# A three-layer kernel on one core: when the side parts of a weight conversion are issued, the order of joined results, and the queue of the row stores

## The chip, the cores and the metric

The kernel runs on one core of one Trainium2 chip. The metric is the device time of one execution in microseconds (us). Before the change it is 578.14 us, the median of three runs (577.61 to 579.5). The profile that is read below comes from one further execution, which took 581.89 us; its span, from the first to the last instruction, is 580.0 us.

## The reference

Three stages follow each other on 1536 tokens of width 512 (two batches of 768). All inputs but the two integers are float32.

```python
scores = q @ k.T / 8 - slope[h] * dist        # 8 heads of width 64, window of 96 + 8 global keys
x = softmax(where(keep, scores, -1e9)) @ v    # [1536, 512]
h = x @ moe_w_in                              # [512, 2048]
x = where(h > 0, h, exp(min(h, 0)) - 1) @ moe_w_out          # [2048, 512]
h = maximum(maximum(x @ moe2_w1, x @ moe2_w2), x @ moe2_w3)  # each [512, 768]
out = h @ moe2_w_out                          # [768, 512]
```

The weights reach the kernel as float64. The kernel turns them into float32 by bit operations and splits each into a high part (a rounded copy) and a low part (the rest), and three matmuls (high by high, high by low, low by high) make one product.

## The kernel before, in words

**Stages.** The tokens go in three blocks of 512 through attention and the first feed-forward layer (`run`). Attention of a later block runs beside the matmuls of the block in front of it. In `run`, the loop over `fc` (16 pieces of 128 hidden columns) does for each `fc`: `product` (12 matmuls into a PSUM bank `h`, L636), the ELU on ACT and DVE (ACT relu and exp, L656 and L657; DVE max, L661), a high part on ACT (`gh`, L643), a low part on DVE (`gl`, L648), and then the out product of the `fc` before it (`out_high`, L667, eight matmuls that read `gh`, and `out_low`, L675, four that read `gl`). So `gh` of one `fc` has the time of one out product and one product (24 matmuls) before PE needs it. The last block has no attention beside it.

**The second layer** (`second`) makes three passes, `p` = 0 to 2. A pass has three keys, `q` = 0 to 2 (the three matrices of the maximum), and then the rows of the out product. A key has `pair` (blocks 0 and 1 joined: seven products of six matmuls each, L905, with sums of operands formed before, in the manner of Strassen and Winograd; results are put together by DVE adds and maxima, `result`, L925 to L934) and `single` (block 2 alone: two products of twelve matmuls, L636). At `q` = 2 each of the six gate tiles is closed: `closed` makes a high part on ACT (L915) and a low part on DVE (L916). Then `rows` goes over 12 rows of 128 tokens: six matmuls each (L997, they read the closed tiles, for rows 0 to 3 the tiles (0,0) and (0,1)), then an ACT copy (pass 0, L1003) or a DVE add of the partial sum of the pass before (L1005), and a store. The partial row is loaded three rows ahead (`fetch`, L986). Row tiles and open gate tiles share seven buffers: row 0 follows on a row of the pass before, rows 1 to 6 each on one gate tile in the order (1,1), (0,0), (0,1), (1,0), (2,0), (2,1), and row 7 and later on the stores of rows 0 and later. PE's products go round eight PSUM banks (`bank`).

**The weight conversion for the second layer** is a generator, `pieces`. Each `next` runs it up to a `yield`, a piece. For each of the 12 groups there are two raw tiles. For a tile: `w_first` (an ACT rescale in place, L475, and a DVE shift, L476), two `w_word` (DVE, L485, each reads what the rescale wrote), `w_split` (ACT high part, L495, and a POOL low part, L496). Three of four groups then form sums: `w_sums` 0 and 1 (two DVE adds each, L508 to L512), with ACT high parts (L515) and POOL low parts (L516) of both. A group of the first kind has 8 pieces, of the other kind 6, 90 in all. Raw tiles come by SP into three buffers; the second raw tile of a group goes into the buffer that the POOL low part of the first sums (L516) of the group before leaves.

**Where pieces are drawn.** In `run`, from `fc` = 9 of the last block: one before the max L661, three at the end of each `fc`, 28 in all. In `second`, by `work(n)` between products, the first four of which are parts of `late` (the split of block 2's tokens, L616 and L617).

Each engine takes its instructions in the order of the program; an ACT instruction that waits for DVE holds all behind it.

```python
e = self.elu_exp(h, n)            # ACT, ACT
...                               # before: a piece here
self.elu_max(e, h)                # DVE
gh = self.high(e, n)              # ACT
gl = self.low(e, gh, n, ...)      # DVE
...                               # pieces here
```

Of the kernel before, what the change touches and what calls it, by code (L numbers as in the profile page):

```python
# [11 lines left out]
F32 = mybir.dt.float32  # L12
F32R = mybir.dt.float32r
# [4 lines left out]
ALU = mybir.AluOpType  # L18
# [5 lines left out]
P = 128  # L24
# [362 lines left out]
class Feed:  # L387
# [80 lines left out]

    def w_first(self, j):

        if j not in self.wraw:
            return
        r = self.wraw[j]
        a = r[:, :, 1].bitcast(F32)
        self.nc.scalar.activation(a, a, AF.Copy, scale=2.0 ** -112)  # L475
        self.nc.vector.tensor_scalar(  # L476
            r[:, :, 0], r[:, :, 0], 29, 1, op0=ALU.logical_shift_right, op1=ALU.bitwise_or
        )

    def w_word(self, j, n):  # L480
        if j not in self.wraw:
            return
        t, a = self.wraw[j][:, :, 0], self.wraw[j][:, :, 1]
        c, op = ((3, ALU.logical_shift_left), (0x80000000, ALU.bitwise_and))[n]
        self.nc.vector.scalar_tensor_tensor(t, a, c, t, op0=op, op1=ALU.bitwise_or)  # L485

    def w_split(self, j):
        if j not in self.wraw:
            return
        nc = self.nc  # L490
        v = self.wraw.pop(j)[:, :, 0].bitcast(F32)
        if j % 2 == 0:
            self.w[j // 2] = self.wt.tile([P, 2, 2, 512], F32R, tag="w", name="w")
        w = self.w[j // 2]
        nc.scalar.copy(w[:, j % 2, 0], v)  # L495
        nc.gpsimd.tensor_tensor(  # L496
            w[:, j % 2, 1], v, w[:, j % 2, 0].bitcast(F32), op=ALU.subtract
        )

    def w_sums(self, j, n):  # L500


        nc = self.nc
        r0, r1 = self.raws[j], self.raws[j + 1]
        v0, v1, t0, t1 = (r[:, :, i].bitcast(F32) for i in (0, 1) for r in (r0, r1))
        a, b = slice(0, 256), slice(256, 512)
        if n == 0:
            nc.vector.tensor_tensor(t1[:, a], v1[:, a], v1[:, b], op=ALU.add)  # L508
            nc.vector.tensor_tensor(t0[:, a], v0[:, a], v1[:, a], op=ALU.subtract)
            return  # L510
        nc.vector.tensor_tensor(t1[:, b], t1[:, a], v0[:, a], op=ALU.subtract)
        nc.vector.tensor_tensor(t0[:, b], v0[:, b], t1[:, b], op=ALU.subtract)  # L512
        w = self.s[j // 2] = self.wt.tile([P, 2, 2, 512], F32R, tag="w", name="ws")
        for u, t in enumerate((t0, t1)):
            nc.scalar.copy(w[:, u, 0], t)  # L515
            nc.gpsimd.tensor_tensor(w[:, u, 1], t, w[:, u, 0].bitcast(F32), op=ALU.subtract)  # L516

    def pieces(self):


        for i in range(2 * NJ):
            j = 2 * (NFC + i)
            while self.nl < min(j + 3, 2 * NFC + 4 * NJ):
                self.w_load()
            self.raws = {j + u: self.wraw[j + u] for u in range(2)}
            for u in range(2):
                self.w_first(j + u)
                yield
                self.w_word(j + u, 0)
                yield  # L530
                self.w_word(j + u, 1)
                self.w_split(j + u)
                if u == 0 or i % 4 == 3:
                    yield
            if i % 4 < 3:
                yield
                self.w_sums(j, 0)
                yield
                self.w_sums(j, 1)
                yield  # L540
            self.made.add(NFC + i)

    def operands(self, y0, y1):
# [183 lines left out]
    def run(self, at, k, x=None, h0=None, aside=None):  # L727
# [3 lines left out]
        nc, ps = self.nc, self.ps  # L731
        nblk = len(BLOCKS)
# [6 lines left out]
        for bi, n in enumerate(BLOCKS):  # L739
            prev = y = None  # L740
            for fc in range(NFC):
                tag = ("h", "S0")[fc % 2] if k >= len(at.steps) + 2 else "h"
# [14 lines left out]
                if bi == nblk - 1 and fc == 2:  # L757
                    sums = self.operands(ysave[0], ysave[1])
# [15 lines left out]
                else:  # L774
# [3 lines left out]
                        at.turn_pe(k - 1)  # L778
                    if not due:
                        at.turn_act(k - 1, nc.scalar.copy)  # L780
                if bi == nblk - 1 and fc > 1:
                    next(sums if fc < 9 else conv, None)
                self.elu_max(e, h)
                if bi == 0:
                    self.c_low(fc + 3)
                if fc == NFC - 1 and bi + 1 < nblk:
                    x = self.split_tiles()
                    t = at.take(g0)
# [37 lines left out]
                    self.c_rebase(fc + 3)  # L826
                    self.w_ahead(min(2 * fc + 4, 2 * NFC - 1))
                if bi == nblk - 1 and fc > 1:
                    for _ in range(1 if fc < 9 else 3):
                        next(sums if fc < 9 else conv, None)  # L830
                k += 1
                prev = gh, gl
            if bi + 1 < nblk:
                self.split_part(x, t, 0, 2, 2, nc.vector)
                for i in range(1, BLOCKS[bi + 1] // GRP):
                    t = at.take(g0 + i)
# [3 lines left out]
            if bi == nblk - 2:  # L840
# [5 lines left out]
                conv = self.pieces()  # L846
# [72 lines left out]
    def pair(self, key, q, g, left, work):  # L919


        nc, o, w, s = self.nc, self.o, self.w[key], self.s[key]
        def add(t, u, tag, pool=self.act):
            out = pool.tile([P, 512], F32, tag=tag, name=tag)
            nc.vector.tensor_tensor(out, t, u, op=ALU.add)  # L925
            return out

        def result(t, u, b, j):
            m = self.gate(g, b, j)
            if q == 0:  # L930
                nc.vector.tensor_tensor(m, t, u, op=ALU.add)
            else:
                c = add(t, u, "c", self.m2)
                nc.vector.tensor_tensor(m, c, m, op=ALU.max)  # L934

        p1 = self.part(w, 0, 0, o["b11"])
        if left:
            self.out_low(*left)
        e1 = self.act.tile([P, 512], F32, tag="e", name="e1", bufs=1)
        nc.scalar.copy(e1, p1)  # L940
        if left:
            self.late = self.save(left[0], left[3])
        p6 = self.part(s, 1, 256, o["t2"])
        u2 = add(p6, e1, "gl")
        work(1)
        p5 = self.part(s, 1, 0, o["t1"])
        v = add(p5, u2, "gh")
        work(1)
        p7 = self.part(s, 0, 0, o["t3"])
        u3 = add(p7, u2, "gl")  # L950
        result(p5, u3, 1, 1)
        result(self.part(w, 0, 256, o["b21"]), e1, 0, 0)
        result(self.part(w, 1, 256, o["t4"]), u3, 0, 1)
        result(self.part(s, 0, 256, o["b22"]), v, 1, 0)
        if q == 2:
            for t in ((1, 1), (0, 0), (0, 1), (1, 0)):
                self.closed(g, *t)
        else:
            work((3, 1)[q])

    def single(self, key, q, g, x, work):
        for u in range(2):
            t = self.bank()
            self.product(t, self.w[key][:, u], x, 512)
            m = self.gate(g, 2, u)
            if q == 0:
                self.nc.scalar.copy(m, t)
            else:
                self.nc.vector.tensor_tensor(m, t, m, op=ALU.max)
            if q == 2:  # L970
                self.closed(g, 2, u)
            work((2 + u, 2, 1)[q])

    def rows(self, p, key, g, parts, work):


        nc, w = self.nc, self.w[key]
        n = NT // P
        last = NJ // 2 - 1
        held = {}  # L980

        def fetch(i):
            if i < n:
                held[i] = self.row("row")
                if p:
                    nc.sync.dma_start(held[i], parts[p - 1][i])  # L986

        for i in range(3):
            fetch(i)
        for i in range(n):  # L990
            fetch(i + 3)
            o = self.bank()
            r = slice(i % 4 * P, i % 4 * P + P)
            for u in range(2):
                t = g[i // 4, u]
                for k, (a, b) in enumerate(((0, 0), (0, 1), (1, 0))):
                    nc.tensor.matmul(  # L997
                        o, t[:, a, r], w[:, u, b],
                        start=u == k == 0, stop=u == 1 and k == 2,
                    )  # L1000
            t = held.pop(i)
            if p == 0:
                nc.scalar.copy(t, o)  # L1003
            else:
                nc.vector.tensor_tensor(t, o, t, op=ALU.add)  # L1005
            dst = self.io["out"][i * P:i * P + P, :] if p == last else parts[p][i]
            (nc.scalar if p == last and i % 2 else nc.sync).dma_start(dst, t)
            if p == 0:
                work(1)


# [287 lines left out]
```

## Time and profile before

| what | us |
|---|---|
| median of three runs | 578.14 |
| the profiled execution | 581.89 |
| its span | 580.0 |
| PE busy | 543.7 (94%) |
| DVE busy | 392.4 (68%) |
| ACT busy | 291.8 (50%) |
| POOL busy | 100.1 (17%) |

PE is busy nearly all the time. What is not used lies in a few places, so the stretches matter and not the shares: the last iterations of block 3, the start of the rows of pass 1, and the end. The second table gives PE's busy time by stretch, from the windows of the trace.

| stretch, us | what runs | length | PE busy |
|---|---|---|---|
| 322 to 373 | last block, `fc` 8 to 15 | 51.0 | 43.32 |
| 373 to 423 | pass 0, three keys | 50.0 | 49.98 |
| 439.4 to 484.4 | pass 1, three keys | 45.0 | 44.98 |
| 484.4 to 491 | rows of pass 1, the start | 6.6 | 1.17 |
| 509 to 553.7 | pass 2, three keys | 44.7 | 44.70 |
| 553.7 to 570.2 | rows of pass 2 | 16.5 | 16.47 |
| 570.2 to 580 | after the last matmul | 9.8 | 0.00 |

### The profile page before, as it was taken

The page shows a single profiled execution, that of the slowest core. Times are in us where ns is not written, and L with a number is a line of the kernel's source. Part 1 is how long each engine was busy: PE and PEld are TensorE (multiplying, and loading weights), DVE is VectorE, ACT ScalarE, POOL GpSimd, SP SyncE. Part 2 cuts the span into 40 slices and gives each one's busy share as a digit, 9 for nine tenths or more (in the row PEclk, how much of TensorE's full clock was granted, in tenths as well). Part 3 has the DMA queues.
Part 4 walks back from the last instruction along what each step waited for, and adds up shares of the span by engine and source line. Part 5 has one row for each costly group of instructions (what it writes and reads, how often), then busy time and mean ns, then how long its engine had stood idle before and what let it go on. Part 6 is the DMA issues. An engine that isn't in the chain of part 4 may idle for free.

```text
span 580.0 us, 7786 instructions
## 1 busy us (share of the span) xinstructions
PE 543.7 (94%) x2718; PEld 428.0 (74%) x2718; DVE 392.4 (68%) x811; ACT 291.8 (50%) x647; POOL 100.1 (17%) x105
## 2 busy tenths in 40 slices
PE   8988999999999999999999998699999996999993
PEld 6556777777777888887888786478878884888882
DVE  6797999999646333343556466678876888677862
ACT  5888777777665555554446455432346323023110
POOL 4100222222210000000000034402324222014000
PEclk8689999999999999999999999899999998999997
DMA  8837444432211111010000012211218324731065
GB/s 303 287 116 294 169 167 169 163 134 77 74 27 40 41 41 42 19 54 1 1 1 1 1 62 84 72 37 37 73 42 268 125 74 133 250 125 55 2 213 209
DMA packets 23583, 59.21 MB, mean 102 GB/s; under 512 B 2544, under 2 KB 2544, under 8 KB 23536
## 3 DMA queue, kind: packets, MB, share of 16 engines
q1 hardware_dynamic: 22672, 57.06, 28.9%
q10 hardware_dynamic: 864, 1.57, 0.7%
q8 instruction: 23, 0.38, 0.3%
q14 instruction: 24, 0.20, 0.1%
HBM read 49.19 MB, written 9.44 MB: 101 GB/s over the span
## 4 chain that ended last, share of the span: by engine, by line
PE 49%; DVE 31%; ACT 12%; issue 4%; DMA 3%; SPq 0%; DVEq 0%; ACTq 0%
PE h L636 13%; PE y L667 9%; DVE wr L449 7%; PE y L675 4%; DVE wr L485 4%; PE y L997 3%; ACT w L457 3%; DVE m L934 3%; PE S L905 3%; PE y L905 3%; PE y L636 2%; DVE c L925 2%; DVE e L661 2%; DMA row<-part 2%; PE TX L315 2%
## 5 line engine op out<-in xcount | busy, mean ns | idle before, releaser
L636 PE MATMUL h<-xh,w 128*128 128x512 f32 (+1 forms) x432 | 115.7, 390 | 0.8 <-ACT xh L616 0.8
L667 PE MATMUL y<-gh,w 128*128 128x512 f32 x384 | 100.7, 405 | 7.7 <-ACT gh L643 7.6
L636 PEld LDWEIGHTS h<-xh,w 128*128 128x128 f32 x432 | 79.1, 188 | 19.6 <-issue 1.7
L667 PEld LDWEIGHTS y<-gh,w 128*128 128x128 f32 x384 | 70.3, 191 | 26.0 <-ACT gh L643 10.4
L661 DVE SCALAR_TENSOR_TENSOR e<-e,h 128x512 f32<-128x512 f32 x48 | 32.9, 686 | 60.1 <-ACT e L657 60.1
L496 POOL TENSOR_TENSOR w<-wr,w 128x512 fp32r<-128x512 f32 x24 | 32.7, 1362 | 227.8 <-ACT w L495 184.9
L636 PE MATMUL h<-xl,w 128*128 128x512 f32 (+1 forms) x216 | 65.8, 386 | 0.0
L263 ACT ACTIVATE p<-p,m 128x232 f32<-128x232 f32 (+1 forms) x96 | 44.8, 468 | 21.6 <-DVE m L242 21.6
L656 ACT ACTIVATE e<-h 128x512 f32<-128x512 f32 x48 | 28.5, 594 | 50.3 <-PE h L636 45.7
L675 PE MATMUL y<-gl,w 128*128 128x512 f32 x192 | 51.6, 390 | 0.0
L485 DVE SCALAR_TENSOR_TENSOR wr<-wr 128x512 uint32<-128x512 uint32 x48 | 41.5, 866 | 13.8 <-ACT wr L475 13.2
L449 DVE SCALAR_TENSOR_TENSOR wr<-wr 128x1024 uint32<-128x1024 uint32 (+1 forms) x36 | 49.9, 1396 | 0.7
L636 PEld LDWEIGHTS h<-xl,w 128*128 128x128 f32 x216 | 40.3, 188 | 8.3
L495 ACT CAST w<-wr 128x512 fp32r<-128x512 f32 x24 | 15.9, 663 | 55.9 <-DVE wr L485 55.9
L643 ACT CAST gh<-e 128x512 fp32r<-128x512 f32 x48 | 29.8, 621 | 26.5 <-DVE e L661 26.4
L675 PEld LDWEIGHTS y<-gl,w 128*128 128x128 f32 x192 | 36.0, 188 | 8.0 <-issue 0.3
L648 POOL TENSOR_TENSOR gl<-e,gh 128x512 fp32r<-128x512 f32 x16 | 21.0, 1313 | 104.9 <-ACT gh L643 104.9
L648 DVE TENSOR_TENSOR gl<-e,gh 128x512 fp32r<-128x512 f32 x32 | 22.2, 692 | 19.9 <-ACT gh L643 19.9
L186 POOL TENSOR_SCALAR raw<-raw,qsc 128x256 f32<-128x256 f32 x24 | 19.0, 791 | 80.3 <-DMA raw<-qk 80.3
L657 ACT ACTIVATE e<-e 128x512 f32<-128x512 f32 x48 | 30.4, 632 | 1.5
L276 DVE TENSOR_SCALAR p<-p,m 128x232 f32<-128x232 f32 (+1 forms) x96 | 28.3, 336 | 1.7
L242 DVE CUSTOM_DVE_ANT_0 p<-S,rel 128x232 f32<-128x232 f32 (+1 forms) x80 | 26.8, 372 | 2.3 <-PE S L216 2.2
(161 smaller groups left out, 912.1 us busy)
## 6 DMA issues: line engine op xcount, KB each, us to landing
wr<-wa SPq DMA_DIRECT2D x14, 1024.0 KB, 7.5
wr<-wb SPq DMA_DIRECT2D x24, 512.0 KB, 3.5
v<-v SPq DMA_DIRECT2D x24, 256.0 KB, 2.7
part<-row SPq DMA_DIRECT2D x24, 256.0 KB, 3.9
row<-part SPq DMA_DIRECT2D x24, 256.0 KB, 4.1
raw<-qk SPq DMA_DIRECT2D x16, 312.0 KB, 3.1
raw<-qk SPq DMA_DIRECT2D x8, 260.0 KB, 3.7
wr<-wa SPq DMA_DIRECT2D x4, 512.0 KB, 3.7
```

The lines of the kernel that those rows point to most:

```text
L263: self.nc.scalar.activation(p[:, o], p[:, o], AF.Exp, bias=m[:, u:u + 1], scale=-1.0, accum_out=m[:, 2 + u:3 + u],)
L449: self.nc.vector.scalar_tensor_tensor(r[..., 0], r[..., 1], v, r[..., 0], op0=op, op1=ALU.bitwise_or)
L485: self.nc.vector.scalar_tensor_tensor(t, a, c, t, op0=op, op1=ALU.bitwise_or)
L496: nc.gpsimd.tensor_tensor(w[:, j % 2, 1], v, w[:, j % 2, 0].bitcast(F32), op=ALU.subtract)
L636: nc.tensor.matmul(out[:, o:n], w[:, part % 2, c * P:c * P + P], (xl if part == 2 else xh)[:, c, o:n], start=c == 0 and part == 0, stop=c ...
L643: self.nc.scalar.copy(gh[:, 0:n], e[:, 0:n])
L648: (engine or self.nc.vector).tensor_tensor(gl[:, 0:n], e[:, 0:n], gh[:, 0:n].bitcast(F32), op=ALU.subtract)
L657: self.nc.scalar.activation(e, e, AF.Exp, scale=-1.0)
L661: self.nc.vector.scalar_tensor_tensor(e, e, -1.0, h, op0=ALU.add, op1=ALU.max)
L667: self.nc.tensor.matmul(y[e][:, 0:n], w[:, a, e * P:e * P + P], g[0][:, 0:n], start=fc == 0 and a == 0, stop=False,)
L675: self.nc.tensor.matmul(y[e][:, 0:n], w[:, 0, e * P:e * P + P], g[1][:, 0:n], start=False, stop=fc == NFC - 1,)
L905: self.nc.tensor.matmul(out, w[:, u, i % 2, b + c * P:b + c * P + P], o[:, i // 2, c], start=c == i == 0, stop=c == 1 and i == 2,)
```

## The change

In `pieces`, the split (ACT and POOL) of a tile is issued with the next piece, not with the second word; the ACT and POOL parts of the sums are issued with the piece behind the second sums. The number of pieces stays the same. In block 3 from `fc` = 9 on, no piece stands before the max; four stand at the end. In `second`, the calls of `work` are shared out otherwise: 12 pieces in place of 10 in `q` = 0, 5 in place of 7 in `q` = 1, 1 in place of 4 in `q` = 2, and four in the rows of pass 1, where there were none. At `q` = 2 the tiles (0,0) and (0,1) are closed before the result (1,0) is formed, then (1,1) and (1,0). The stores of the rows of passes 0 and 1 move from SP's queue to ACT's; in pass 2, where even rows went by SP and odd ones by ACT, all go by ACT but row 11. Three tests for a tile that isn't there go away.

```diff
-        w = self.s[j // 2] = self.wt.tile([P, 2, 2, 512], F32R, tag="w", name="ws")
-        for u, t in enumerate((t0, t1)):
-            nc.scalar.copy(w[:, u, 0], t)
-            nc.gpsimd.tensor_tensor(w[:, u, 1], t, w[:, u, 0].bitcast(F32), op=ALU.subtract)
+        else:
+            w = self.s[j // 2] = self.wt.tile([P, 2, 2, 512], F32R, tag="w", name="ws")
+            for u, t in enumerate((t0, t1)):
+                nc.scalar.copy(w[:, u, 0], t)
+                nc.gpsimd.tensor_tensor(
+                    w[:, u, 1], t, w[:, u, 0].bitcast(F32), op=ALU.subtract
+                )
...
                 self.w_word(j + u, 1)
+                yield
                 self.w_split(j + u)
-                if u == 0 or i % 4 == 3:
-                    yield
             if i % 4 < 3:
-                yield
                 self.w_sums(j, 0)
                 yield
                 self.w_sums(j, 1)
                 yield
+                self.w_sums(j, 2)
             self.made.add(NFC + i)
...
-                if bi == nblk - 1 and fc > 1:
-                    next(sums if fc < 9 else conv, None)
+                if bi == nblk - 1 and 1 < fc < 9:
+                    next(sums, None)
...
-                    for _ in range(1 if fc < 9 else 3):
+                    for _ in range(1 if fc < 9 else 4):
...
         u2 = add(p6, e1, "gl")
-        work(1)
+        work((3, 1, 0)[q])
         p5 = self.part(s, 1, 0, o["t1"])
         v = add(p5, u2, "gh")
-        work(1)
+        work((2, 0, 0)[q])
...
+        if q == 2:
+            self.closed(g, 0, 0)
+            self.closed(g, 0, 1)
         result(self.part(s, 0, 256, o["b22"]), v, 1, 0)
         if q == 2:
-            for t in ((1, 1), (0, 0), (0, 1), (1, 0)):
-                self.closed(g, *t)
-        else:
-            work((3, 1)[q])
+            self.closed(g, 1, 1)
+            self.closed(g, 1, 0)
+        work((2, 1, 0)[q])
...
-            work((2 + u, 2, 1)[q])
+            work((2 + u, 1 + u, u)[q])
...
-            (nc.scalar if p == last and i % 2 else nc.sync).dma_start(dst, t)
-            if p == 0:
+            (nc.sync if p == last and i > n - 3 and i % 2 else nc.scalar).dma_start(dst, t)
+            if p == 0 or (p == 1 and i % 3 == 2):
                 work(1)
```

## Rows read from the trace of the kernel before

**Rows 1.** Windows: stretch, length, busy us by engine, PEclk, DMA share, GB/s.
```profile
322.00:373.00 51.00, 43.32 (x185) 33.90 (x184) 31.23 (x50) 26.44 (x44) 16.22 (x12) 0.99 0.15 46
439.40:484.40 45.00, 44.98 (x199) 36.92 (x197) 36.93 (x56) 16.63 (x29) 16.32 (x13) 1.00 0.36 122
484.40:491.00 6.60, 1.17 (x3) 0.74 (x4) 6.19 (x10) 2.47 (x4) 1.31 (x1) 0.81 0.65 202
491.00:496.00 5.00, 5.00 (x14) 3.90 (x14) 3.63 (x8) 1.82 (x3) 0.00 (x0) 0.56 0.50 153
553.70:570.20 16.50, 16.47 (x73) 13.32 (x71) 8.45 (x14) 1.24 (x2) 0.00 (x0) 1.00 0.78 274
570.20:580.00 9.80, 0.00 (x0) 0.00 (x0) 1.94 (x3) 0.00 (x0) 0.00 (x0) 0.69 0.38 139
```

**Rows 2.** PE's waits from 300 us on: total us, times, longest us.
```profile
PE y L667 <- ACT gh L643: 7.6, 5, 4.6
PE S L997 <- DVE g L916: 2.9, 1, 2.9
PE S L997 <- ACT g L915: 2.6, 1, 2.6
PE TX L997 <- DVE g L916: 0.2, 1, 0.2
```

**Rows 3.** Timeline of block 3's end: start, us, engine, instruction, [idle before].
```profile
331.82 0.69 DVE L648 TENSOR_TENSOR gl<-e,gh 128x512 fp32r<-128x512 f32 x1 [0.69 <-ACT gh L643]
...
345.48 0.69 DVE L648 TENSOR_TENSOR gl<-e,gh 128x512 fp32r<-128x512 f32 x1 [0.69 <-ACT gh L643]
...
369.00 1.21 ACT L515 CAST ws<-wr 128x512 fp32r<-128x512 f32 x2 [1.90 <-DVE wr L512]
...
370.11 0.60 ACT L656 ACTIVATE e<-h 128x512 f32<-128x512 f32 x1
...
372.78 0.69 DVE L648 TENSOR_TENSOR gl<-e,gh 128x512 fp32r<-128x512 f32 x1 [0.68 <-ACT gh L643]
```

**Rows 4.** Groups by line: count, busy us, mean ns of one, idle before.
```profile
L485 DVE SCALAR_TENSOR_TENSOR wr<-wr 128x512 uint32<-128x512 uint32 x48 | 41.5, 866 | 13.8 <-ACT wr L475 13.2
...
L516 POOL TENSOR_TENSOR ws<-wr,ws 128x512 fp32r<-128x512 f32 x18 | 24.6, 1385 | 20.7 <-ACT ws L515 19.1 <-issue 1.6
...
L476 DVE TENSOR_SCALAR wr<-wr 128x512 uint32<-128x512 uint32 x24 | 11.9, 497 | 2.6 <-DMA wr<-wb 2.6
...
L512 DVE TENSOR_TENSOR wr<-wr 128x256 f32<-128x256 f32 x9 | 8.8, 976 | 0.3
```

**Rows 5.** Page, DMA issues: count, KB each, us to landing.
```profile
wr<-wb SPq DMA_DIRECT2D x24, 512.0 KB, 3.5
```

**Rows 6.** Timeline of pass 1, end of the third key and start of the rows.
```profile
478.99 0.69 DVE L925 TENSOR_TENSOR gl<-S,e 128x512 f32<-128x512 f32 x1 [1.20 <-ACT e L940]
...
490.56 2.08 PE L997 MATMUL S<-w,g 128*128 128x512 f32 x4 [2.87 <-DVE g L916]
...
492.43 2.77 PE L997 MATMUL TX<-w,g 128*128 128x512 f32 x6
```

**Rows 7.** Timeline of the last rows, pass 2.
```profile
554.77 0.69 DVE L916 TENSOR_TENSOR g<-m,g 128x512 fp32r<-128x512 f32 x1 [0.69 <-ACT g L915]
...
556.75 0.69 DVE L916 TENSOR_TENSOR g<-m,g 128x512 fp32r<-128x512 f32 x1 [0.69 <-ACT g L915]
...
558.46 0.92 SPq L986 DMA_DIRECT2D row<-part  x2
...
568.65 1.52 PE L997 MATMUL y<-w,g 128*128 128x512 f32 x6
...
574.18 0.69 DVE L1005 TENSOR_TENSOR row<-y,row 128x512 f32<-128x512 f32 x1
```

**Rows 8.** DMA issues from 553 us on: count, KB each, us to landing.
```profile
row<-part SPq DMA_DIRECT2D x9, 256.0 KB, 4.5
...
out<-row ACTq DMA_DIRECT2D x6, 256.0 KB, 4.2
```

More of the change, by code (lines that the diff above doesn't have):

```diff
@@ L469, in w_first @@
     def w_first(self, j):
-        if j not in self.wraw:
-            return
         r = self.wraw[j]
@@ L480, in w_word @@
     def w_word(self, j, n):
-        if j not in self.wraw:
-            return
         t, a = self.wraw[j][:, :, 0], self.wraw[j][:, :, 1]
@@ L487, in w_split @@
     def w_split(self, j):
-        if j not in self.wraw:
-            return
         nc = self.nc
@@ L509, in w_sums @@
             nc.vector.tensor_tensor(t0[:, a], v0[:, a], v1[:, a], op=ALU.subtract)
-            return
-        nc.vector.tensor_tensor(t1[:, b], t1[:, a], v0[:, a], op=ALU.subtract)
-        nc.vector.tensor_tensor(t0[:, b], v0[:, b], t1[:, b], op=ALU.subtract)
-        w = self.s[j // 2] = self.wt.tile([P, 2, 2, 512], F32R, tag="w", name="ws")
-        for u, t in enumerate((t0, t1)):
-            nc.scalar.copy(w[:, u, 0], t)
-            nc.gpsimd.tensor_tensor(w[:, u, 1], t, w[:, u, 0].bitcast(F32), op=ALU.subtract)
+        elif n == 1:
+            nc.vector.tensor_tensor(t1[:, b], t1[:, a], v0[:, a], op=ALU.subtract)
+            nc.vector.tensor_tensor(t0[:, b], v0[:, b], t1[:, b], op=ALU.subtract)
+        else:
[5 more added lines that the diff above has]
+                )
     def pieces(self):
```

## The prediction

> **What bounds the kernel now.** I read the windows by stage first [rows 1]: PE is the bound, and it is full in the keys of the passes (44.98 of 45.0 us in pass 1) and in the last rows (16.47 of 16.5). It has idle time in three places only: 51.0 - 43.32 = 7.7 us at the end of block 3, 6.6 - 1.17 = 5.4 us where pass 1 goes over to its rows, and 9.8 us behind the last matmul. Then PE's waits [rows 2], which say for whom it waited: in block 3 for `gh` on ACT (7.6 us in 5 waits, the longest 4.6), in pass 1 for the closed tiles (2.9 and 2.6), in pass 0 for the same tiles 0.2. Last the timelines of these places [rows 3, 6, 7], for what held those engines. So the change is worth what it does at three places: the conversion in block 3, the close of pass 1, and the tail. Elsewhere an earlier ACT or DVE gains nothing, since PE has no gap there.
>
> **Block 3.** The sum goes from `gh` to `gh`, since `gl` (L648) starts as `gh` is ready. Before, `gh` is ready at 331.82, 345.48 and 372.78 [rows 3], 13.65 us for two `fc`; PE alone needs 10.9 (48 matmuls of 0.227, from six in 1.36, shown as 1.52 with the last one's end [rows 7]). So ACT and DVE set this stretch already, and PE waits at its end: relu (L656) starts at 370.11 since ACT sat behind the casts of the sums, which wait for L512 [rows 3].
>
> After, two `fc` have 4 pieces each, all behind `gl`. Take T as the time at which `gh` is ready.
> First kind (`fc` = 11, 13, 15). ACT issues two sums' casts (1.2 [rows 3]), the rescale of the first tile (taken as one cast, 0.6), its cast, the rescale of the second tile, and only then the next relu. DVE runs `gl`, a shift, two words, a shift. The words collide with the POOL parts of the sums, so the pair of words, which takes 2 x 0.87 = 1.7 on average [rows 4], ends at about T + 4.4 and the cast at T + 5.0. The second tile has to be loaded by then. Its buffer is free when POOL has done its first sum: 0.75 (cast and hand-over) + 1.39 [rows 4] gives T + 2.1; the load takes 3.5 [rows 5], so T + 5.6. With the rescale and hand-overs relu starts at T + 6.3. From relu's start to `gh` it is 372.78 - 370.11 = 2.7 us [rows 3]: this kind takes 9.0. `fc` = 9 has no sums in front; there the cast ends at T + 3.0, relu starts at 3.5, 6.2 in all.
> Second kind (`fc` = 10, 12, 14). ACT has one cast, behind `gl` and two words: relu at T + 2.6, exp done at 3.85. DVE still has the sums, with L512 beside POOL, until T + 4.6; max and `gh` then take 1.3: 5.9 in all.
> The first pair takes 6.2 + 5.9 = 12.1 in place of 13.65, a gain of 1.5; the two later pairs 14.9 in place of 13.65, a loss of 2.5. **Term 1: +1.0 us.** Bounds: if the load is in time the first kind takes 8.3, which makes -0.5; if the idle time of PE, now in two parts of about 3 us, costs it its clock twice, which cost 2.2 us in pass 1 (below), +3.2.
>
> **The close of pass 1.** PE is done with the third key at 484.4 and starts the rows properly at 490.56 [rows 6], 6.2 us late, when the low part of (0,0) is there. What goes away ahead of it on DVE:
> - Pieces: counted through block 3 (28), pass 0, its rows and pass 1, 76 conversion pieces stand ahead of the third key's results before and 71 after. The five are a shift (0.50), two words (1.73) and two sums (0.98 for L512 alone) [rows 4], at least 3.2 us.
> - Order: before, the low part of (0,0) comes behind the add and the max of (1,0) and the low part of (1,1), three DVE instructions of 0.69 [rows 6]: 2.0 us.
> - ACT: `e1` stood behind a cast that waited for words; DVE waited 1.2 us for it [rows 6]. No piece stands there at `q` = 2 any more.
> That makes 6.4 against 6.2. The second tile's low part is wanted 0.68 later (three matmuls) and takes 0.69, so the margin is about nothing. I leave 0.3 us of the wait.
> The clock: in 484.4 to 491 the granted clock is 0.81 and in 491 to 496 it is 0.56 [rows 1], that is partly at the lower of 1.2 and 2.4 GHz, behind 5.4 us with 1.17 us of work. The ten matmuls at 490.56 and 492.43 end at 495.0, 4.4 us for what takes 2.27 at the full clock [rows 6]. With no wait of that kind this 2.2 us comes back.
> **Term 2:** 5.4 + 2.2 - 0.3 = **-7.3 us**, and -0.2 for the same wait in pass 0 [rows 2]. Bounds: nothing left, -7.6; half of the idle time and of the slow clock left, -3.7. The pieces taken from `q` = 1 and 2 go to `q` = 0 (two more) and the rows of pass 1 (four); there DVE had 6.19 of 6.6 us only at the start [rows 1], and in pass 2, where nothing waits, PE's eight banks hide a late DVE. Cover gone: see the slower rival.
>
> **The tail.** The last rows' matmuls end at 568.65 + 1.52 = 570.2 and the last add at 574.18 + 0.69 = 574.9 [rows 7]; 5.1 us follow until 580.0 (store and end). Rows 4 and 5 are loaded from 558.46 on [rows 7], though their buffers, gate tiles, are free by then: that of row 6, the last closed, at 557.4, that of row 5 at 555.5 [rows 7], that of row 4 ahead of it. On SP they stand behind the store of row 0, which waits for its add. So all later loads are late, and DVE waits for them.
> After, SP has loads alone. Rows 4 and 5 go at about 554.5 and 555.5, row 6 at 557.5. Row 11 follows on the store of row 4: its matmuls end at 560.6, the add at 561.3, the store is issued within 0.4 and lands 4.2 later [rows 8], 565.9; the load takes 4.5 [rows 8], 570.4. Its add then ends at 571.1 in place of 574.9. **Term 3: -3.8 us.** Bounds: PE's end allows 571.0 at best, -3.9; with loads as late as now 0. On ACT the stores wait for DVE's adds, and behind them stand pieces and the next `e1`; in pass 2 nothing. In pass 1 the add of row 11 ends about 1 us behind the last row's matmuls, ahead of `e1`'s product, so that wait costs nothing. In pass 0 the store follows ACT's own copy.
> The Trainium skill speaks against this term: in DMA: Bandwidth & Descriptors, section Issuing engines are not separate DMA queues, it says that transfers of several engines run on the same 16 DMA engines, and that issuing from several saves only the time of issuing. By that the sum would be without this term, -6.5. The rows show the DMA engines at 0.78 and 274 GB/s there [rows 1], not full over the stretch, and what is late is the issue.
>
> **Sum.** 1.0 - 7.3 - 0.2 - 3.8 = -10.3 us. Against the profiled execution, 581.89 (1.89 outside the span), this gives 571.6. That execution lies 3.75 above the median of the runs, so I take the difference over: 578.14 - 10.3 = **567.8 us**. The three tests taken out act while the program is written and cost nothing.
>
> **Rivals.**
> 1. The close of pass 1 stays half late, because the twelve pieces of `q` = 0 keep DVE behind and the sums' casts come a piece later. For it: the margin above is 0.2 us. Against: five pieces fewer is a lower bound. Then -3.7 in place of -7.3: 571.4.
> 2. The tail is bound by the transfers: twelve loads and twelve stores of 256 KB are 6.3 MB in some 20 us, and the queue is shared. For it: a load takes 4.5 there, against 3.5 for twice the bytes elsewhere [rows 5, 8]. Against: the share of 0.78. Then term 3 falls away: 571.6. This is also what the rule of the Trainium skill above would give.
> 3. Slower: twelve pieces in `q` = 0 of passes 1 and 2 push DVE so far behind that PE runs out of its eight banks. At `q` = 2 of pass 1 `u2` starts at 478.99, some 7 us behind its product. From a lag of 10.9 us (eight products of 1.36) on PE waits. If each of the twelve pieces cost 1.8 us (the word at twice its mean), `q` = 0 would take 12 x 1.8 + 7 adds x 0.69 = 26.4 against 15.0 of PE: with the 6 us of lag it has, some 6 us of waiting in each of the two passes, while the close stays as late as it is: 578.1 + 1.0 + 12 - 3.8 = 587. Against: ten pieces there gave no wait.
> 4. It does not do what it says: casts a piece later wait as long, since ACT takes the next piece at once; the close and the tail keep their waits: 578 to 579.
>
> **How the numbers follow.** Chances: as worked out 0.64 (its own range 564.5 to 570.5), rival 1 0.13, rival 2 0.11, rival 3 0.06, rival 4 0.06. Some 0.3% (1.7 us) is what a measurement can tell from no change. Faster by more takes the forecast and rivals 1 and 2, and a little of 4: 0.89; within 0.05; slower 0.06. The range reaches from 563.5 (all lower bounds: -0.5 - 7.8 - 3.9 = -12.2, and some 2 us for places not counted) to 573.5 (both rivals 1 and 2 in part, or term 1 at its upper bound beside one of them).
>
> **What would show it.** Term 1: `gh` of the last `fc` about 1 us later than at 372.78, with relu behind a rescale that waits for a load. Term 2: no wait of L997 in pass 1 over 0.5 us, no window at half clock behind 484 us, `u2` of the third key within 2 us of its product. Term 3: row loads in a run without stores between them on SP, the last add within 1.5 us of the last matmul. The prediction fails if PE waits for a bank or a weight in passes 1 or 2, if block 3 ends over 3 us later, or if DVE still waits for row loads at the end by more than 2 us.

## The result, and the profile after

The changed kernel takes 570.98 us (median of four runs, 570.36 to 572.5) against 577.93 of the kernel before on the same chip: a ratio of 0.9878, 95% interval 0.9852 to 0.9905, or some 7 us less. The forecast was 567.8, in a range of 563.5 to 573.5. So the direction and the range held, but of 10.3 us worked out only 7 came. The ratios here and below are taken from the undisturbed runs of both kernels on one chip, so they need not be the quotient of the medians (e2, e4, g1 and g2 differ most), and on the chip of g1 and g2 the kernel before took 576.4 to 579.7 us in five executions and 583.3 to 584.2 in six.

The profiled execution took 570.36 us with a span of 568.5. Its 11.5 us less of span are not all the change's: `gh` of `fc` = 9 is ready at 327.56 in place of 331.82 [rows 3], and up to there both kernels run the same instructions, but for one piece that the kernel before draws ahead of that `gh`. The granted clock of the first 60 us was 0.97 here and 0.86 there. That part varies by as much between the profiled executions of all these kernels (327.3 to 335.2 us until `gl` of `fc` = 9 starts), so below the traces are compared from `gl` of `fc` = 9 on, in four stretches: to the first matmul of the passes, to PE's last matmul, to the last add, to the end of the span.

| us | block 3 from `fc` 9 | passes | PE's end to last add | rest | sum |
|---|---|---|---|---|---|
| before | 44.36 | 193.99 | 4.70 | 5.13 | 248.2 |
| changed | 44.43 | 186.12 | 4.55 | 5.84 | 240.9 |

The passes gave 7.9 us, block 3 nothing, and the time behind PE's end grew by 0.6. Windows of the changed kernel (stretch, length, busy us by engine, granted clock, DMA share, GB/s); its lines are some numbers lower than before's (L667 is L663, L916 is L912, L997 is L995, L1005 is L1003, L485 is L481).

```profile
327.60:372.00 44.40, 38.39 (x153) 30.41 (x153) 30.65 (x45) 21.98 (x37) 16.50 (x11) 0.92 0.14 48
478.80:485.00 6.20, 5.46 (x23) 3.88 (x22) 5.52 (x9) 2.38 (x5) 0.00 (x0) 1.00 0.37 110
485.00:490.00 5.00, 5.00 (x23) 4.14 (x23) 4.07 (x8) 1.99 (x4) 1.55 (x1) 1.00 0.63 182
541.60:558.10 16.50, 16.50 (x73) 13.32 (x71) 10.54 (x17) 2.14 (x4) 0.00 (x0) 1.00 0.76 243
558.10:568.50 10.40, 0.01 (x1) 0.00 (x0) 2.77 (x4) 0.00 (x0) 0.00 (x0) 0.71 0.54 202
```

The second and third line answer to the start of the rows of pass 1 [rows 1]: PE is idle for 0.74 us in place of 5.4, and the clock stays at full speed. The last line, the time behind the last matmul, is 10.4 us long in place of 9.8. PE's waits from 300 us on, which answer to [rows 2]:

```profile
PE y L663 <- ACT gh L639: 6.6, 4, 2.9
PE S L995 <- DVE g L912: 0.7, 1, 0.7
```

The chain that ended last in the changed kernel shows what the tail is made of (start, us, what; pieces under 0.1 us left out):

```profile
551.66 0.12 DVE row L1003
551.78 4.31 DMA out<-row
556.15 5.63 DMA row<-part
561.97 0.69 DVE row L1003
```

The add of row 4 ends at 551.78, its store lands 4.31 us later, only then row 11 can be loaded into the same buffer, 5.63 us, and its add is the last. PE had finished row 11 at 558.1. In the kernel before the chain went another way, over SP's queue: the loads of rows 4 and 5 stand there behind the store of row 0, and that of row 10 behind the store of row 6 (SPq L1007 issues a store, SPq L986 a load):

```profile
558.07 0.34 SPq L1007
...
558.46 0.42 SPq L986
...
565.80 0.42 SPq L1007
...
566.31 7.04 DMA row<-part
```

The last two loads there, of rows 10 and 11, took 7.0 and 7.2 us, not the 4.5 of the median over the tail [rows 8].

### The profile page after: what moved, and what is told of

Its sections match the earlier page's. It is cut to its first block, busy times and chain, and to the rows that moved or that the text cites. A ratio compares the mean times of both kernels' runs of the same rounds, so it can differ in the third digit from the quotient of the medians.

```text
span 568.5 us, 7773 instructions
## 1 busy us (share of the span) xinstructions
PE 537.3 (95%) x2718; PEld 425.2 (75%) x2718; DVE 398.9 (70%) x811; ACT 290.9 (51%) x647; POOL 104.2 (18%) x105
## 4 chain that ended last, share of the span: by engine, by line
PE 38%; DVE 34%; ACT 13%; DMA 6%; issue 5%; POOL 2%; ACTq 0%; DVEq 0%; SPq 0%
PE h L632 14%; PE y L663 9%; DVE wr L449 7%; PE y L671 5%; DMA wr<-wb 4%; DVE wr L481 3%; ACT w L457 3%; DVE c L921 3%; DVE m L930 3%; DVE e L657 2%; DVE p L242 2%; ACT wr L438 2%; PE TX L292 2%; DVE gl L921 2%; PE TX L315 2%
## 5 line engine op out<-in xcount | busy, mean ns | idle before, releaser
L663 PE MATMUL y<-gh,w 128*128 128x512 f32 x384 | 100.8, 405 | 6.6 <-ACT gh L639 6.6
L663 PEld LDWEIGHTS y<-gh,w 128*128 128x128 f32 x384 | 70.4, 191 | 24.1 <-ACT gh L639 8.5
L481 DVE SCALAR_TENSOR_TENSOR wr<-wr 128x512 uint32<-128x512 uint32 x48 | 47.8, 995 | 12.6 <-ACT wr L473 11.4
L652 ACT ACTIVATE e<-h 128x512 f32<-128x512 f32 x48 | 28.5, 594 | 50.3 <-PE h L632 45.7
L511 POOL TENSOR_TENSOR ws<-wr,ws 128x512 fp32r<-128x512 f32 x18 | 28.8, 1616 | 32.0 <-ACT ws L510 22.8
```

The source lines that it names most:

```text
L663: self.nc.tensor.matmul(y[e][:, 0:n], w[:, a, e * P:e * P + P], g[0][:, 0:n], start=fc == 0 and a == 0, stop=False,)
```

## The experiments

Each kernel was timed against the kernel before on its chip; the medians take all of its runs. The segments of its trace, cut as above, and the time by which the last gate tile of pass 2 is closed (its L912 or L916 ends) ahead of PE's end:

| kernel | median us | ratio [95%] | block 3 | passes | to last add | rest | last close ahead |
|---|---|---|---|---|---|---|---|
| before | 577.9 | | 44.36 | 193.99 | 4.70 | 5.13 | 12.7 |
| changed | 570.98 | 0.9878 [0.9852, 0.9905] | 44.43 | 186.12 | 4.55 | 5.84 | 9.4 |
| e1 before, stores on ACT | 576.55 | 0.9964 [0.9931, 0.9997] | 44.55 | 195.60 | 0.72 | 5.71 | 12.7 |
| e2 changed, stores as before | 573.38 | 0.9876 [0.9828, 0.9924] | 45.59 | 187.94 | 5.94 | 5.27 | 9.4 |
| e3 changed, ten row buffers | 568.27 | 0.9803 [0.9757, 0.9848] | 44.75 | 185.89 | 1.37 | 6.30 | 10.0 |
| e4 changed, 12 pieces in rows | 580.12 | 1.0003 [0.9967, 1.0040] | 44.26 | 196.41 | 0.83 | 5.92 | 12.6 |
| f1 before, new order | 575.76 | 0.9962 [0.9931, 0.9993] | 44.27 | 191.67 | 3.53 | 5.08 | 12.6 |
| f2 before, new shares | 572.57 | 0.9897 [0.9850, 0.9943] | 44.42 | 188.43 | 4.86 | 5.19 | 11.1 |
| f3 before, parts later | 580.29 | 1.0031 [1.0008, 1.0054] | 44.16 | 193.76 | 3.61 | 5.19 | 11.8 |
| f4 changed, block 3's old places | 566.49 | 0.9817 [0.9762, 0.9871] | 40.33 | 184.97 | 4.73 | 5.66 | 9.3 |
| g1 f4 and ten row buffers | 566.27 | 0.9749 [0.9693, 0.9806] | 40.93 | 186.16 | 2.38 | 6.66 | 9.4 |
| g2 g1 and 6 pieces in rows | 563.67 | 0.9721 [0.9658, 0.9784] | 40.79 | 186.35 | 0.72 | 5.78 | 12.6 |
| h1 changed, 6 pieces in rows | 567.54 | 0.9830 [0.9776, 0.9884] | 45.45 | 185.36 | 0.79 | 6.15 | 12.4 |
| h2 changed again | 570.86 | 0.9871 [0.9828, 0.9913] | 44.04 | 185.98 | 4.57 | 5.95 | 9.5 |

Stretches that no edit touches differ by up to 1.6 us between executions (the passes of e1 and before, block 3 of h1 and changed), so a difference of that size in one trace says nothing by itself. In e1's passes it goes with the clock: the granted clock is 0.50 from 484 to 488 us and 0.54 from 488 to 494, lower for longer than in the kernel before [rows 1], while the waits there are much the same (5.1 and 5.4 us).

**e1, the stores alone.**

```diff
-            (nc.scalar if p == last and i % 2 else nc.sync).dma_start(dst, t)
+            (nc.sync if p == last and i > n - 3 and i % 2 else nc.scalar).dma_start(dst, t)
```

> The kernel before with one part of the change alone: the row stores on ACT's queue. Theory (the tail is the chain from the add of row 4 over its store to the load of row 11 and its add, since rows share seven buffers; in the changed kernel DVE closes the gate tiles of pass 2 3.3 us later against PE, so row 4 is added late and the gain is lost): here DVE closes as early as before, row 4 is added at PE's pace, and the last add comes about 1.4 us behind PE's end in place of 4.7, so some 3.3 us less: 574.6. Rival (the end is bound by the transfers, whatever queue issues them): no change, 577.9.

The last add comes 0.72 us behind PE's end, PE's own pace. The end of its timelines, PE's last matmuls and DVE's last adds:

```profile
566.25 1.52 PE L997 MATMUL y<-w,g 128*128 128x512 f32 x6
```
```profile
566.44 0.69 DVE L1005 TENSOR_TENSOR row<-TX,row 128x512 f32<-128x512 f32 x1 [0.62 <-DMA out<-row]
567.80 0.69 DVE L1005 TENSOR_TENSOR row<-y,row 128x512 f32<-128x512 f32 x1 [0.67 <-PE y L997]
```

The last add waits for PE here, not for a load. So the stores on ACT do what the prediction worked out, 4.0 us to the last add (3.4 with the rest of the span), though the same bytes are moved. The time fell by less: 576.55 lies between the theory's 574.6 and the rival's 577.9, and the interval allows 0.2 to 4 us. SP's queue in this run, all ten loads in a row with no store between them:

```profile
549.90 13.70 SPq L986 DMA_DIRECT2D row<-part  x10
```

Counted from PE's end, the loads of rows 4 to 6 are issued 16.7 to 12.7 us ahead of it, where it was 11.7 to 10.2, and the load of row 11 takes 4.24 us in place of 7.21. So 3.0 of the 4.0 us are a shorter last load. That loads which were held back run beside the later ones and slow them is the likely reason; no run takes it by itself.

**e2, the stores undone in the changed kernel.** The edit is that of e1 the other way round.

> The changed kernel with the row stores on the queues of before. Theory: with DVE's closes 3.3 us later than before and loads behind stores again, the last add comes 7 to 8 us behind PE's end in place of 4.6: some 3 us more than the changed kernel, 574. Rival (transfers bind): as the changed kernel, 571.

The last add comes 5.94 us behind PE's end, not 7 to 8, against 4.55 in the changed kernel, and DVE's close is as late as there. The time decides nothing: the median, 573.38, lies 2.4 us above the changed kernel's, but measured against the kernel before in the same batch of runs the two are alike, 0.9876 and 0.9878. By the one trace the stores earned about 1.4 us of tail in the changed kernel, not 4. There is a second difference, in `q` = 1 of pass 2, where PE waits for banks that DVE and ACT have not emptied:

```profile
PE h L901 <- DVE m L927: 0.8, 1, 0.8
PE y L632 <- ACT e L936: 0.6, 1, 0.6
```

The changed kernel has no such wait.

**e3, ten row buffers.**

```diff
-                held[i] = self.row("row")
+                if p == last and 6 < i < 10:
+                    held[i] = self.cv.tile([P, 512, 2], F32, tag="wr", name="rx").rearrange(
+                        "p c w -> p (c w)"
+                    )[:, 0:512]
+                else:
+                    held[i] = self.row("row")
```

> The changed kernel; rows 7 to 9 of pass 2 go into the three raw buffers of the conversion, which are idle by then, so that only rows 10 and 11 wait for a store (of rows 0 and 1). Theory: the chain over row 4's store is cut, the last add comes within 1.5 us of PE's end in place of 4.6: some 3 us less, 568. Rival (transfers bind): 571, with the DMA engines as full as now and the loads landing as late.

The last add comes 1.37 us behind PE's end in place of 4.55, and the time is 568.27. Rows 7 to 9 wait for no store here, rows 10 and 11 for those of rows 0 and 1 in place of 3 and 4, and 3.2 us of the tail go, though the same bytes are moved. That speaks against the rival a second time.

**e4, a piece in every row of pass 1.**

```diff
-            if p == 0 or (p == 1 and i % 3 == 2):
+            if p < 2:
```

> The changed kernel with a piece drawn in every row of pass 1 in place of every third (12 in place of 4), so that 6 conversion pieces are left for pass 2 in place of 14. Theory: DVE is in time in pass 2, the gate tiles close some 3 us earlier against PE, row 4 is added earlier, and the last add comes 2 us behind PE's end in place of 4.6: some 2.3 us less, 568.7; if the wait for stores is the whole of it whatever DVE does, 571. Rival (transfers bind): 571.

The tail came as the theory had it, 0.83 us: DVE closes 12.6 us ahead of PE's end again. The time didn't: the ratio to the kernel before is 1.0003. PE's waits from 480 us on in this kernel:

```profile
PE S L901 <- DVE row L1003: 5.9, 1, 5.9
PE h L901 <- DVE m L927: 2.3, 1, 2.3
PE S L995 <- DVE g L912: 0.7, 1, 0.7
```

PE wants a bank for the fifth product of pass 2 (L901) that DVE has not emptied, since its adds of the rows (L1003) stand behind pieces, and in `q` = 1 one that still holds a result of `q` = 0 (L927). With these 8.2 us of waiting goes a granted clock of 0.51 from 509 to 516 us. That is the mechanism of the slower rival of the prediction, brought about by twelve pieces in the rows of pass 1. Seen with this run alone, the short tail could also come from PE having been held up; h1 settles that.

**f1, the order of results and closes alone.**

```diff
+        if q == 2:
+            self.closed(g, 0, 0)
+            self.closed(g, 0, 1)
         result(self.part(s, 0, 256, o["b22"]), v, 1, 0)
         if q == 2:
-            for t in ((1, 1), (0, 0), (0, 1), (1, 0)):
-                self.closed(g, *t)
+            self.closed(g, 1, 1)
+            self.closed(g, 1, 0)
```

> The kernel before with the new order of results and closes alone ((0,0) and (0,1) closed ahead of the result (1,0)). By the steps of the prediction this takes 2.0 of the 6.2 us by which the rows of pass 1 start late; the rest of the wait stays and with it most of the slow clock: 2 to 3 us less, 575.5. Rival (the order is the whole of it): 570.5, no wait left. Rival (order counts for nothing since DVE is as late): 578.

PE waits 3.3 and 0.7 us at the rows of pass 1, 4.1 in all in place of 5.4, and the passes take 2.3 us less. The expected 2.0 was not quite reached: the way from `u2` to the close of (0,0) is 2.1 us shorter, but `u2` itself starts 0.8 us later against PE in this execution.

**f2, the shares of the pieces alone.** The edit is the five calls of `work` of the change.

> The kernel before with the new shares of pieces alone (12, 5, 1 and four in the rows of pass 1). By the steps of the prediction 3.2 + 1.2 of the 6.2 us go and 1.8 stay, too short for a lower clock; the last close of pass 2 comes 3 us later against PE, as in the changed kernel, and with the stores on SP the last add comes some 5.9 us behind PE's end in place of 4.7: -4.4 - 2.2 + 1.2 = -5.4, 572.8. Rival (the shares do little by themselves, the head of ACT's queue matters): the wait stays at 5 us or more, 577 to 579.

1.8 us of waiting is left at the rows of pass 1, and 1.1 at those of pass 2; the passes take 5.6 us less, the time is 572.57. This is the largest single part of the gain. The 1.8 was met in the sum and not item by item: the wait of DVE for `e1` ahead of `u2`, 1.2 us, which the expectation counts as gone, is still there, and the pieces gave more than their 3.2.

**f3, the parts of ACT and POOL a piece later, alone,** with block 3's four pieces at the end of an iteration.

> The kernel before with the parts of ACT and POOL issued with the next piece, and block 3's four pieces behind the low part, alone. Theory: in block 3 gh of the last fc comes 1.0 to 1.5 us later against fc 9, but the end of the block does not move by more than 0.5, as in the changed kernel; in pass 1 ACT holds fewer heads, but the number of pieces ahead of the close stays, so the wait of 5.4 us stays by more than half: 576 to 578.5. Rival (this part carries the gain of pass 1): no wait left in pass 1, 570.5.

Alone it makes the kernel slower, by 0.31% [0.08%, 0.54%], and 580.29 lies outside the expected 576 to 578.5. PE still waits 2.9 and 1.3 us in pass 1, and block 3 is as long as before. The trace from `fc` = 9 on shows no loss of that size, so where it comes from stays open; it is about the size of what these executions vary by.

**f4, block 3's pieces where they stood before,** the rest as changed.

```diff
-                if bi == nblk - 1 and 1 < fc < 9:
-                    next(sums, None)
+                if bi == nblk - 1 and fc > 1:
+                    next(sums if fc < 9 else conv, None)
...
-                    for _ in range(1 if fc < 9 else 4):
+                    for _ in range(1 if fc < 9 else 3):
```

> The changed kernel with block 3's pieces where they stood before (one ahead of the max, three at the end), the parts of ACT and POOL still a piece later. Theory: the first kind of iteration then has the casts of the sums ahead of gh, which makes gh 1.2 us later there, and the load starts earlier by as much; block 3 ends within 1 us of the changed kernel: 571. Rival (the new places in block 3 are worth a gain of their own): 573 or more.

The expectation missed: block 3 takes 40.33 us in place of 44.43, and the time is 566.49. ACT's and DVE's waits in block 3 of the changed kernel:

```profile
DVE wr L474 <- DMA wr<-wb: 3.0, 2, 1.9
ACT wr L473 <- DMA wr<-wb: 1.6, 2, 1.2
```

In f4 there is no such wait. With a piece ahead of the max the casts of the sums come ahead of `gh`, POOL frees the raw buffer that much earlier, and the load of the second tile is there in time:

```profile
337.59 1.23 ACT L510 CAST ws<-wr 128x512 fp32r<-128x512 f32 x2 [0.34 <-DVE wr L506]
337.81 0.68 DVE L657 SCALAR_TENSOR_TENSOR e<-e,h 128x512 f32<-128x512 f32 x1
...
339.30 0.60 ACT L639 CAST gh<-e 128x512 fp32r<-128x512 f32 x1
339.69 1.60 SPq L421 DMA_DIRECT2D wr<-wb  x2
...
343.42 0.66 ACT L473 ACTIVATE wr<-wr 128x512 f32<-128x512 f32 x1
343.98 0.58 ACT L652 ACTIVATE e<-h 128x512 f32<-128x512 f32 x1
```

ACT's casts of the sums run beside DVE's max, work that costs `gh` little; relu (L652) starts behind a rescale (L473) that waits for nothing. The load that relu depends on is issued 0.4 us behind the start of `gh` here and lands 3.1 later; in the changed kernel it is issued 2.9 us behind it and lands 4.1 later. In the kernel before, the casts of the sums wait 1.9 us for DVE and relu stands behind them; in f4 they wait 0.3 to 0.8, and relu is ahead of them. So the later parts by themselves gain 4.0 us in block 3 (44.36 to 40.33), and the new places give that away again. Of the 4.0, `gh` of the last `fc` is 2.6 earlier against `fc` = 9; the other 1.4 are the eight matmuls behind it, which ran at the full clock here. In g1 and g2, with the same places, they did not, and the block took 40.93 and 40.79.

**g1, f4 and e3 together.**

> The changed kernel with the two edits that made it faster together: rows 7 to 9 of pass 2 in the idle raw buffers, and block 3's pieces where they stood before. If they act in different places, their gains add: block 3 ends 4 us earlier (against fc 9) and the last add comes within 1.5 us of PE's end: 566.5 - 3.0 = 563.5. If the tail was bound by the transfers after all once the rest is faster, 566.5.

The time is the one that was put down for the rival (566.5), not 563.5. Block 3 keeps its gain; the last add comes 2.38 us behind PE's end, in place of 4.73 in f4 but not 1.5 at most, and the rest takes 1.0 longer than in f4. Some transfers are slower, with the early loads of rows 7 to 9 beside them: the store of row 1, which row 11's load waits for, takes 4.8 us, where it took 3.0 in the changed kernel. The medians of g1 and f4, 566.27 and 566.49, were taken on different chips; against the kernel before beside it, it is 2.5% faster [1.9%, 3.1%], f4 1.8% [1.3%, 2.4%]. Whether the buffers gain anything on top of f4 is not told by that.

**g2, the same with six pieces in the rows of pass 1.**

```diff
-            if p == 0 or (p == 1 and i % 3 == 2):
+            if p == 0 or (p == 1 and i % 2 == 1):
```

> The same, and in the rows of pass 1 a piece is drawn in every second row in place of every third (6 in place of 4). Theory: DVE closes pass 2 earlier by some 1 us, which no longer counts with ten row buffers, and the rows of pass 1 can't hold much more on DVE (with 12 pieces PE waited 5.9 us for a bank there): 563 to 565, no gain over the kernel without it. Rival (DVE's lateness in pass 2 still binds): 562.

It takes 563.67 us, in the expected range, but the reason given was wrong in part: DVE's lateness did still count, since the last add now comes 0.72 us behind PE's end, with the last close 12.6 us ahead in place of 9.4. This is the lowest median of all, 2.8% [2.2%, 3.4%] below the kernel before; the intervals of f4 and g1 overlap with it.

**h1, six pieces in the rows alone,** the edit of g2 on the changed kernel, **and h2, the changed kernel again.**

> The changed kernel with one edit: in the rows of pass 1 a piece in every second row in place of every third (6 in place of 4). Theory (the gain of the stores was lost to DVE's lateness in pass 2): the last close comes 12.5 us ahead of PE's end in place of 9.4, the last add within 1.5 us of it in place of 4.6, with seven row buffers and no wait for a bank: 3 us less than the changed kernel. Rival (the seven buffers bind by themselves, and the run with all 12 pieces had a short tail only since PE had been held up): the last add stays 3 us or more behind PE's end, time as the changed kernel.

> The changed kernel once more, for comparison on the same chip: last add 4.5 us behind PE's end, some 1.2% below the kernel before.

On one chip h2 takes 570.86 and h1 567.54; the intervals of their ratios overlap, so the size rests on the traces. h1's last adds, with seven buffers:

```profile
548.00 1.28 DVE L1003 TENSOR_TENSOR row<-S,row 128x512 f32<-128x512 f32 x2
...
550.98 0.69 DVE L1003 TENSOR_TENSOR row<-y,row 128x512 f32<-128x512 f32 x1 [0.51 <-PE y L995]
...
558.61 0.69 DVE L1003 TENSOR_TENSOR row<-S,row 128x512 f32<-128x512 f32 x1 [0.89 <-DMA row<-part]
559.22 0.68 DVE L1003 TENSOR_TENSOR row<-TX,row 128x512 f32<-128x512 f32 x1
560.56 0.69 DVE L1003 TENSOR_TENSOR row<-y,row 128x512 f32<-128x512 f32 x1 [0.66 <-PE y L995]
```

The add of row 4 waits for PE here (550.98, 0.51 us), the chain over its store starts as early as PE allows, and the last add waits for PE again. PE waits for no bank. Two pieces moved from pass 2 to the rows of pass 1, and nothing else, take the tail from 4.57 to 0.79. In the traces DVE begins the results of `q` = 1 in pass 2 1.7 us earlier against PE, and two words fewer stand behind that (1.2 us): 2.9 us at the last close.

## Why the prediction was right, and where it failed

**Block 3** was right within its bounds. `gh` of the last `fc` was put 1.0 us later against `fc` = 9 and came 1.5 later; the three pairs of iterations took 12.3, 15.5 and 14.7 us where 12.1, 14.9 and 14.9 were worked out. Relu stood behind a rescale that waited for a load, as was said. The timeline (start, us, engine, instruction, [idle before]), which answers to [rows 3]:

```profile
346.24 0.68 ACT L473 ACTIVATE wr<-wr 128x512 f32<-128x512 f32 x1 [1.24 <-DMA wr<-wb]
...
346.81 0.59 ACT L652 ACTIVATE e<-h 128x512 f32<-128x512 f32 x1
...
349.49 2.62 PE L663 MATMUL y<-gh,w 128*128 128x512 f32 x8 [2.87 <-ACT gh L639]
...
364.15 3.47 PE L663 MATMUL y<-gh,w 128*128 128x512 f32 x8 [1.87 <-ACT gh L639]
...
370.03 2.12 PE L663 MATMUL y<-gh,w 128*128 128x512 f32 x8 [1.27 <-ACT gh L639]
```

The eight matmuls at 349.49 and 364.15 ran partly at the lower clock, in time that PE had to spare; those of the last `fc` took 2.12 us where they had taken 3.54, so that the end of the block moved by 0.1 and not by 1.0. That was partly luck: in e2 and h1, whose block 3 is the same, the block took 45.59 and 45.45. What the sum didn't see is f4: that the one part of the change loses here what another gains.

**The close of pass 1** was right in its size and its parts, less so in its way. 7.3 + 0.2 us were worked out; the passes gave 7.9, 0.7 us of waiting stayed where 0.3 was left for it, and the lower clock is gone from there. f1 and f2 show both parts to count, and the shares more: alone they take 1.4 and 3.6 us off the wait. But the sign that `u2` of the third key would start within 2 us of its product was not met. The product ends at 466.9 and `u2` starts 6.4 us behind it, where it was 6.8:

```profile
473.31 0.68 DVE L921 TENSOR_TENSOR gl<-S,e 128x512 f32<-128x512 f32 x1
```

So what was taken away ahead of the third key brought DVE only 0.4 us forward, with two words that took 2.5 us right ahead of `u2`; the gain came behind it: the low part of (0,0) starts 6.5 us after `u2` in place of 10.8. Rival 1 is out. The rival that the change does not do what it says is out with it.

**The tail** failed: 3.8 us were worked out, and the stretch behind the last matmul is 0.6 longer. The step that failed is the add of row 4, put right behind its matmuls ("its matmuls end at 560.6, the add at 561.3"). In the trace PE has row 4 done at 548.6, and the add runs from 551.07 to 551.78, 2.5 us later than it would be by that step, since DVE closes the last gate tile until 548.75, 9.4 us ahead of PE's end and not 12.7 as before [rows 7], and then adds rows 0 to 6 one behind the other (rows 3 to 6 in the second line):

```profile
548.06 0.69 DVE L912 TENSOR_TENSOR g<-m,g 128x512 fp32r<-128x512 f32 x1 [0.69 <-ACT g L911]
...
550.47 2.48 DVE L1003 TENSOR_TENSOR row<-y,row 128x512 f32<-128x512 f32 x4
```

The last add was put 0.9 us behind PE's end and came 4.55 behind it. Of these 3.6 us the late add makes 2.5, and the load of row 11 1.1 (5.63 where 4.5, the median of the tail, was taken); the store, 4.31, was as put (4.2). Why DVE is late there is shown by h1 and e4: the new shares draw three pieces fewer in the keys of pass 0 and three fewer in those of pass 1, and put back four in the rows of pass 1, which leaves 14 conversion pieces for pass 2 where 12 were. They don't do it alone: in f2, with 14 pieces and nothing else changed, the last close comes 11.1 us ahead of PE's end, in f3, with the later parts alone, 11.8, and with both 9.4. The prediction counted these pieces for pass 1 and said of pass 2 that nothing waits there but the banks. The wait was there: row buffers, held by rows that DVE adds late. By the prediction's own signs this term failed: DVE waits 5.4 us in the tail for row loads (4.1 for loads, 1.3 for the chain over the store of row 4), over the 2 us that it names.

**The sum.** By the two traces the terms came to +0.1, -7.9 and +0.6 where +1.0, -7.5 and -3.8 were put. The measured 570.98 lies closer to rivals 1 and 2 (571.4 and 571.6) than to the forecast, though neither is what happened, as the runs show and the time alone could not. That the range held is in part luck: its upper end was made for those rivals and for term 1, not for a late add of row 4.

The rule of the Trainium skill in DMA: Bandwidth & Descriptors, section Issuing engines are not separate DMA queues, seemed to fit the result, since the tail did not move. e1 speaks otherwise: with the same bytes on the same engines, moving the issue alone took the last add from 4.70 to 0.72 us behind PE's end. What it saved was not the time of issuing but the wait of loads behind stores that themselves waited for an add, and with it the length of the last loads (7.0 and 7.2 us before, 4.2 for that of row 11 in e1). The rule says nothing of such waits, so the two don't contradict each other; using it as a bound on the gain would have been wrong. Rival 2, that the bytes set the end whatever issues them, is out by e1, e3 and h1; that transfers slow each other at the end is not out, and would be part of the tail. Rival 3's mechanism is real: PE waits for banks in `q` = 0 and 1 of pass 2, 8.2 us in e4, with twelve pieces in the rows of pass 1, and 1.5 in e2; with the change as it is, it waits for none.

## What to carry to other kernels

Where work is moved out of a stretch that waits, count what is left for each later stretch and look there for a buffer that its lateness would hold; here two pieces made DVE 2.9 us later and decided over 3.8 us of tail (h1 against h2). A gain that is absent is not a gain that was never there: undo or do each part alone before giving up on it, since a part can be worth nothing only because of another one beside it. And where an instruction of one engine frees a buffer for a load, issuing it a step later also moves the load.

## What the runs showed of the hardware that was not expected

How long PE runs at its lower clock in the first 60 us is worth as much as the change. `gl` of `fc` = 9, up to which these kernels are alike, starts at 327.3 to 327.7 us in the five profiled executions with a granted clock of 0.97 in that stretch, at 328.6 to 328.9 in the five with 0.94, at 329.7 in h1 with 0.91, and at 331.8 and 332.3 in the two with 0.86. f3, the latest, 335.2, is no exception, though its figure is 0.91 too: its clock records begin only at 24.2 us, and from 10 to 20 us PE ran 53 matmuls there, as few as the 56 of the kernel before at 0.53, where the changed kernel ran 80 at 1.00. A difference of two profiled spans is therefore not the effect of an edit until this stretch is taken out.

PE's clock fell in the changed kernel's block 3 though PE worked in between: the granted clock was 1.00 from 348 to 350 (PE idle for 1.5 of 2 us), 0.72 and 0.50 in the next two windows of 2 us, with PE busy throughout, at the lower of 1.2 and 2.4 GHz:

```profile
348.00:350.00 2.00, 0.52 (x2) 0.47 (x3) 1.23 (x2) 0.68 (x2) 0.00 (x0) 1.00 0.00 0
350.00:352.00 2.00, 2.00 (x8) 1.53 (x8) 1.93 (x5) 0.48 (x1) 0.00 (x0) 0.72 0.00 0
352.00:354.00 2.00, 2.00 (x6) 1.56 (x5) 1.97 (x4) 1.32 (x3) 1.51 (x1) 0.50 0.00 0
```

In f4, with PE waiting 4.8 us in all in that stretch where the changed kernel waits 6.0, the granted clock stays at 1.00. The waits alone don't tell which it will be. g2 has the same waits as f4, to 0.05 us, and behind the last and longest (3.2 us in both) its clock fell:

```profile
366.00:368.00 2.00, 2.00 (x8) 1.58 (x7) 1.97 (x3) 0.00 (x0) 0.58 (x1) 0.76 0.71 258
```

In the same way a wait of 1.96 us in block 3 was followed by a granted clock of 1.00 in the kernel before (359 to 361 us) and of 0.61 in f1 (356 to 358), in the same instructions. So block 3's length in one trace holds a part that no edit made.
